# The first block of a fused chunk attention: keys stored once in a row, sums by a column of ones, a new order table

## The chip, the cores and the metric

One core of a Trainium2 chip runs the whole program in one launch. The metric is the device time of one execution in microseconds; three executions of the kernel before give a median of 1080.98 us.

## What is computed

The reference is an attention over chunks, followed by two MLPs, all in float32:

```python
for c in range(768 // 32):
    k_full = concat([mem_k, k[32 * c - 16 : 32 * c + 40]])     # 8 memory keys, up to 56 of the sequence
    v_full = concat([mem_v, v[32 * c - 16 : 32 * c + 40]])
    a = softmax(q[32 * c : 32 * c + 32] @ k_full.T / 8)
    out[32 * c : 32 * c + 32] = a @ v_full
x = out as 3072 tokens x 512
x = silu(x @ w_in) @ w_out            # 512 -> 2048 -> 512
x = relu(x @ w2_in) ** 2 @ w2_out     # 512 -> 2048 -> 512
```

There are 4 batches, 8 heads and a head size of 64. Neighbouring chunks share keys: a chunk sees 16 keys to its left, its own 32, 8 to its right, and the same 8 memory keys as every other chunk of its head.

## The kernel before

**Tiling.** The 3072 tokens are 6 blocks (j) of 512. A block's attention is done in 4 units (p), each of one pair of heads and 16 chunks. The first MLP runs over 16 tiles (i) of 128 hidden units; every float32 matrix is held as a high part and a rest, and three matmuls make one product. Blocks 0 and 1 take the plain form: `hidden` (12 matmuls, L1204 to L1206), silu on ACT, the split of the result, and `back` (12 matmuls, L1263 to L1265). Later blocks and the second MLP use forms with fewer products.

**The start.** Block 0 can't begin its MLP before its four attention units have made x and before the weights of tile 0 have been loaded and converted. A weight tile comes as 64-bit words; `words` (L849) takes them apart with two ACT instructions (L858, L863) and two DVE instructions (L867, L873), then ACT makes the high part (L956) and DVE or POOL the rest (L960). W(i,0) below is the words of tile i of the input matrix, W(i,1) those of the output matrix, 512 KB each.

**A first unit** (`attend_first`, `soften`, `weigh_first`, `norm_first`) works on a pair of heads a = 0, 1 at once. Keys and values lie in block form: a tile of [128 partitions, 2, width], in which partition rows of the other head are zero. So each half is first cleared by a memset (`clear`, L573) and then filled by a DMA over every other partition (`fill_block`, L582). For the keys the width is 16 chunks x 64 = 1024 columns: every chunk has its own copy of all its 64 keys, memory included. For the values it is 16 x 64 = 1024 columns. The sums of the softmax come from 7 small products against a tile `heads` of [128, 2, 2], loaded by a DMA of its own (L547), and are read with the values' results by three DVE instructions (L780 to L784). PE turns the scores and the results by matmuls with an identity `ident`, which has a pool of its own.

**Holding back.** W(1,0), W(2,0) and the raw inputs of block 1 are not loaded at once: a one-column copy on POOL (`room`, L911, L480) writes into their buffers first, and reads x of unit 0 or 1, so that the load waits for that x. All loads are issued by SP, in its program order.

**The order.** Every piece of work is a `Piece` with the engines that may do it. The order of all pieces, and the engine of each (V, A, G for DVE, ACT, POOL), stands in a table written out by hand, `ORDER` (L88): each word is a step in the list of pieces. An engine runs its pieces in that order; waits follow from the data and from buffers that are used again.

Of the kernel before, what the change touches and what calls it, by code (L numbers as in the profile page):

```python
# [12 lines left out]
F32 = mybir.dt.float32  # L13
# [12 lines left out]
GC = 4  # L26
# [19 lines left out]
ZERO = {"DVE": 1.1, "POOL": 1.2, "ACT": 1.0}  # L46
# [42 lines left out]
0V 1 3 11 -10G 2A 1 -2 10V 2A -1 2 -10 11 7G -6A 8A 1 -4 2 -25 7V 2V 1 33G 1 -36 34 -13V -10 1V 1  # L89
56 -32A 1 -35V 23V -12V 31V -22V 1 16A -49A 36 -7 5V 3A 1 17 1A -5A -1 -19 21 41 -31V 1 -24V 1 1A  # L90
23A -22V 43G 1 -7A 1A 38 -70 9 -4V 17V 1 1A -14V 1 1A 49 -28V 1V 1A -22V 40G 1 -18G 244G 1 1G -265
8 -7V 8V 272G -258A -1A 2V 6A -28 27A -19 -7A 1V 322 -301V 302 1 -317A 1V 317 -63 -206 8 -42A 1V
12A -1A 2V 1V -10V 303 -4A 5 -303V 3 232 -192 261 -68V -226A 295 -6A 1V -289G 299 -296A 223V 1V
-237A 51 254A -304G 237V -226A 235 -225A -8V 292A -277A -14V 6A -3 289V -7 -281 -3A 7V 5A 38 -49V
293A -286V 12A 22 250 -278V -5A 6V 280A -274A -11V 47 -29A 268V 2 -282A 6V -4 9A -10V 49 -43V 14A
-1A -7V 204 -209A 199 -185V 261A -2 -272V 199A -151 -43V 9V -8A 2 192 75A -266 -2V 49 -41A 263 -2V
-258A -2G 185V -182A 7A 176V -139 -36A -7V 257 2A -207 -44V -7V 66 -58V -7A 181 77A -257V 260
-253A 251V -178 -79 180A -173G 2A 172V 83 -254A 9A -1A -7V 44 205A -240V 6A -14V 249A -240V 164
-170 19A -18 246V -4 -236A 176 -185A 10G 163V -161A 162V 12 -158A -8A 155V 1V -175G 251A -75 -120
199 -234V 156A -155V -9V 1V 9A 155 -161 235A -228V -9A 234 -70V -153A -10G 164V 73V -218A 1A 220A  # L100
-228V 153 -144V 223 -231V 153A -144V -6 225A -224 150V -153A 228V -4 -212A -11G 12A -4A 5V 7A -11V
10A 136 -141V 12A 15 193 -213V -4 213A -74V 12 -153A 7V 209A -74V -141G 19A 123V 74V -4 -201A 142
-10V -123A -8V -5A 26 -12V 198A -211V 18A 191 -195V 5A -14V 207A -180 -17A 5V -12 -2A 3 204V -197G
120 79 -78A -130V 14V 3 -2A 4A 112 -115V 4A 193 -81V 77A -175 -13V 112V -107A -4V 112 -107A 180
-72A -94 -13V -5A 113V 74A -186G 190A -3V -176A 104 -110V 7A 182 -186 108V -110A 19 -12V 178A -182
108V -110G 215 -104V -100A 174V -173A 169 -69V 76A -163 -18V 182A -176V -5A 182V -181G 10A 94 103
-30 -166A -6V 100A -80 -13V 1V -7A 177 -175 6A -7V 10A -2V 3A 1V 13 74 78A -164V 162 -75V -84 1
-3A 87V 77A -163G 4A 160V -77 -82A 161 -78A -82V 12 -7A 78V -77A -5V 6V -5A 178 -19A -153V 151 33
-30A -159V 6A 172V 12 -30V -153G 3A 169V -168A 169V -18 -154 173V -169V 170A -169V 301V -298 456
-309A -146 166V 132G -131 -170A 150A 27 -176V 458A -308V -4 53 260A -282V 283V -145 -137V -8 9V -8  # L110
-20 29V -8 9A -8 147 -13V 1V 154 -310A 2V 2A -3 29V -27 28 -26 310 -4A 1A -306V 30 280A -3V -306
142G 160 8A -269 -11V 113G 168V -286 119G -118 5V -4 118G -117 4V 281 -167 11A -10 -114 117V 12A
# [12 lines left out]
-112V 10A -9V 5A -3 30V -22A 23V -162 241A -106V 5V 103 -247 5V -4 1 138V -137 287 -284V 144A -4G
100V 2A -97G -144V 242A -97 -7V -137 242V -97A -6G 95 23 -117V 19V -13V 2 -1 -6V 19V -11A 115 3
-2A -102 -13V 116V -265 160V -159 1 159V -158 275 -11A -104 105A 11 -129 109A -108 118V 1V 12 -25A
1V 36 -22A 1V 116 -94 -12V -131A 1G 108A 24V 11 -292A 280V -22G -2G 37 -142 -1 132V 14A -13A 15V
-60 59 -3 1 16 -44V 3A 34 -20V -12A -1G 29A -27V 41 -2A -311V 284 17V 11G 13 -10A -1A 12 -28 18V
1V 10 -86A -3A 1V 5 56 4A 34 1 -33A 13A -1V 10V -86G 143 -78V 33 1 -33A 13A -73A 75A -3G -35 44V  # L130
-20V -23 81 -80 62 -61 42V -8V 9 -26V 37 -93V -4A 1G 108 -22 1 1 1 -33 66A -44V 45V 1 12 -11A 1A
11 -10G -22A 23G 12 1V 11 -22A 13V -14G -25A 162 -113 -21A -33A -2A 45V 2V -13V 2G 30 -9 1 -54A
-1V 2V 4V -8V 47A -11A 1V 21 -49V 39V -29 75 3 12 -60 46A 3A 2V -4V 14 -9V -2A 3V 9 11 -110A -1A
59 53 46 -156V 1V 89A 1G -38A -7A 46A -44A 63 -12V 1V 12 -65G 91 -88A -71A 70V -12 1 1 55A -54 -31
42V 62 -20V 2V 44A 2 1A 1A -3V -160V 173 1 -53V -99G 1V 1V 50A 4A 86V -89V 90V -138 95 55 12 1
-165G 142A 1G -140 95 162 -151A 44V 2V -1V 2V -15V -30A 33A 1V 21 1 -54A -62V 63V -2V 34A 1V -48 1
1 56A 1V -48G 94 3 12 1 -166A 1V 2V -1V 149A 3A 2V -51 9 41A 12 -61 72 1 1 1 -176V 147V -45 -100A
-3G 4G 1 99 1 59V 1V -121A 111A -149A 1V 2 -1 195 -47V -3V -151V 111A 1V 1A 1V 69 -74A 1V 66 -24G
-144A 1V 34V -33 1 144A 1V 1A 27A 2 1A 1A 1G -25V 1 -7V -146A 1V 185 1 3 12 -11V 2V -1V 2V -191 -1
275 -97A 1G -16A 38 -36A -13 1 1 17G 5G 1G -22 -114 161 1 -36A 1G -4V 2V 38 -11A -13A 2A 29 1A 2  # L140
12 1 -11A -33V -2V 13V 19V 2A 2V -61A 1V -111 174A -25 -153A 1A 58 117G 10 1V 1V 1V 1 44 -55G -2G
-175V 161A 1V 33 1 1 1 -33A -164V 165V 12A -15A 1V 15V -176A 1A 1V 175A 26 1A 2 20 1 -20A 1A 22 12
-64V -175V 193 13V -60 -90 127 1 -132A 95 1 1 -148V 2V 199V -149A 1V 196A -248G 207A -2G 21V 1V 1V
21V -247G 206G -25 -179 1 179 158 -104 -29A -15A -2A 47 -10V 1A 10 -44A 57V -200V 140V 2V 15V
-147A 1V 133V -142A 1A 1V 2V 196 -197V 148V 52 12 -210V 1V 195A 3A -48A 49A -48V 59 -58A -210 62
-59 235 31 71 -93V -19V 52 1 1 -34V -19 54 -13V -207A 4A -8G 152G 73 -72A 2A 37V -183G 1 180V -179
215 -69A -3G 58V 15V 3 -74G 73 3 1 -2 -108A 1V 34V 22A -9 1 1 -168V 190V 18V -32V 53 1 -53A -8 54
8 1 -53A 30 -31V -176 -1 179V 53 -39V 3A -2V 1V 2V 1A 1V 58 3 12 1 -73A 1V 57A 3A 2G -1A -3V 5V
# [1910 lines left out]
```

## Time and profile before

| | |
|---|---|
| median of three executions | 1080.98 us (1080.51 to 1084.42) |
| profiled execution, own time | 1079.09 us |
| its span in the profile | 1077.1 us |
| mean granted clock of PE | 0.998 |
| bytes moved by DMA | 257.66 MB |

The span is from the first to the last instruction on the engines; the own time has 1.99 us more around it. PE is the tensor engine's matmuls, PEld its weight loads, DVE, ACT and POOL the other three engines, SP the engine that issues DMAs. The granted clock PEclk is a share of 2.4 GHz. Matmuls are pipelined, so that a busy PE is not one at its peak.

### The profile page before, as it was taken

The page shows a single profiled execution, that of the slowest core. Times are in us where ns is not written, and L with a number is a line of the kernel's source. Part 1 is how long each engine was busy: PE and PEld are TensorE (multiplying, and loading weights), DVE is VectorE, ACT ScalarE, POOL GpSimd, SP SyncE. Part 2 cuts the span into 40 slices and gives each one's busy share as a digit, 9 for nine tenths or more (in the row PEclk, how much of TensorE's full clock was granted, in tenths as well). Part 3 has the DMA queues.
Part 4 walks back from the last instruction along what each step waited for, and adds up shares of the span by engine and source line. Part 5 has one row for each costly group of instructions (what it writes and reads, how often), then busy time and mean ns, then how long its engine had stood idle before and what let it go on. Part 6 is the DMA issues. An engine that isn't in the chain of part 4 may idle for free.

```text
span 1077.1 us, 24974 instructions
## 1 busy us (share of the span) xinstructions
PE 1064.3 (99%) x9857; PEld 976.9 (91%) x9857; DVE 826.7 (77%) x1610; ACT 604.8 (56%) x1110; POOL 252.8 (23%) x232
## 2 busy tenths in 40 slices
PE   7999999999999999999999999999999999999998
PEld 5787777778888888988999999999999999999998
DVE  6877757677978888888888877677777777677766
ACT  4998854556766777767576534335335334335333
POOL 1122123123333333410201231221222123122110
PEclk9999999999999999999999999999999999999999
DMA  8967687979798888786665767667577577567675
GB/s 276 342 216 220 228 283 234 305 232 313 234 303 294 281 279 290 269 310 222 231 210 197 252 207 228 193 210 232 186 214 240 177 210 241 187 203 237 191 222 170
DMA packets 139748, 257.66 MB, mean 239 GB/s; under 512 B 12272, under 2 KB 52336, under 8 KB 139632
## 3 DMA queue, kind: packets, MB, share of 16 engines
q1 hardware_dynamic: 139632, 256.07, 73.1%
q8 instruction: 78, 1.28, 0.5%
q14 instruction: 38, 0.31, 0.1%
HBM read 203.59 MB, written 52.43 MB: 238 GB/s over the span
## 4 chain that ended last, share of the span: by engine, by line
PE 94%; DMA 2%; ACT 1%; SPq 1%; DVE 1%; issue 0%; POOL 0%; ACTq 0%; DVEq 0%; POOLq 0%
PE out L1598 37%; PE pp L1416 22%; PE ph L1204 8%; PE ph L1206 8%; PE ph L1205 8%; PE acc L1263 3%; PE acc L1265 3%; PE acc L1264 2%; PE po L740 1%; PE sc L516 1%; DMA y<-y 1%; DMA i<-weights 1%; DMA blocks<-head 0%; DMA turned<-bounce 0%; PE turned L633 0%
## 5 line engine op out<-in xcount | busy, mean ns | idle before, releaser
L1416 PE MATMUL pp<-xs,forms 128*128 128x256 f32 x2016 | 273.5, 281 | 0.0
L1598 PE MATMUL out<-w,g 128*128 128x256 f32 x2016 | 272.5, 283 | 0.0
L1598 PEld LDWEIGHTS out<-w,g 128*128 128x128 f32 x2016 | 255.6, 191 | 0.0
L1416 PEld LDWEIGHTS pp<-xs,forms 128*128 128x128 f32 x2016 | 253.4, 189 | 0.0
L1474 ACT CAST g<-sums 128x512 fp32r<-128x512 f32 x240 | 147.5, 619 | 122.5 <-PE out L1598 103.9
L1478 DVE TENSOR_TENSOR g<-sums,g 128x512 fp32r<-128x512 f32 x201 | 153.8, 770 | 45.3 <-ACT g L1474 44.1
L1598 PE MATMUL out<-g,w 128*128 128x256 f32 x1344 | 172.0, 283 | 0.0
L1598 PEld LDWEIGHTS out<-g,w 128*128 128x128 f32 x1344 | 166.0, 188 | 4.6
L1433 ACT ACTIVATE sums<-pp 128x256 f32<-128x256 f32 x192 | 73.8, 384 | 165.1 <-PE pp L1416 124.0
L1459 POOL TENSOR_TENSOR sums<-sums 128x256 f32<-128x256 f32 x59 | 50.5, 860 | 274.4 <-DVE sums L1459 220.3
L1204 PE MATMUL ph<-x,i 128*128 128x512 f32 x240 | 95.8, 399 | 1.3 <-DVE xq L751 0.9
L1205 PE MATMUL ph<-x,i 128*128 128x512 f32 x240 | 94.7, 395 | 0.0
L1206 PE MATMUL ph<-x,i 128*128 128x512 f32 x240 | 94.7, 395 | 0.0
L1452 DVE SCALAR_TENSOR_TENSOR sums<-sums 128x256 f32<-128x256 f32 x144 | 69.1, 485 | 25.5 <-ACT sums L1433 23.8
L1459 DVE TENSOR_TENSOR sums<-sums 128x256 f32<-128x256 f32 x181 | 76.2, 439 | 10.3 <-ACT sums L1556 7.5
L1478 POOL TENSOR_TENSOR g<-sums,g 128x512 fp32r<-128x512 f32 x39 | 50.8, 1305 | 107.6 <-ACT g L1474 107.5
L1655 ACT CAST w<-w 128x512 fp32r<-128x512 f32 x100 | 59.5, 619 | 25.5 <-PE out L1598 18.4
L1661 DVE TENSOR_TENSOR w<-w,w 128x512 fp32r<-128x512 f32 x85 | 63.0, 765 | 8.3 <-ACT w L1655 7.6
L1204 PE MATMUL ph<-x,d 128*128 128x512 f32 x144 | 57.6, 400 | 0.0
L1206 PE MATMUL ph<-x,d 128*128 128x512 f32 x144 | 56.8, 395 | 0.0
L1205 PE MATMUL ph<-x,d 128*128 128x512 f32 x144 | 56.8, 395 | 0.0
L1442 DVE TENSOR_TENSOR sums<-pp,sums 128x256 f32<-128x256 f32 x96 | 40.3, 420 | 21.3 <-PE pp L1416 20.4
(140 smaller groups left out, 1568.0 us busy)
## 6 DMA issues: line engine op xcount, KB each, us to landing
w<-w2s SPq DMA_DIRECT2D x120, 512.0 KB, 4.0
w<-w1s SPq DMA_DIRECT2D x32, 768.0 KB, 5.1
w<-w2s SPq DMA_DIRECT2D x96, 256.0 KB, 3.2
wraw<-weights SPq DMA_DIRECT2D x44, 512.0 KB, 5.1
raw<-units SPq DMA_DIRECT2D x20, 768.0 KB, 5.6
w2s<-ws SPq DMA_DIRECT2D x56, 256.0 KB, 3.2
raw<-units SPq DMA_DIRECT2D x20, 520.0 KB, 5.5
bounce<-squares SPq DMA_DIRECT2D x32, 256.0 KB, 3.4
```

Source lines behind the costliest of these rows:

```text
L1204: nc.tensor.matmul(o, w[:, 1, ws], x[:, 0, kt], start=(kt == 0), stop=False)
L1205: nc.tensor.matmul(o, w[:, 0, ws], x[:, 1, kt], start=False, stop=False)
L1206: nc.tensor.matmul(o, w[:, 0, ws], x[:, 0, kt], start=False, stop=(kt == KT - 1))
L1416: nc.tensor.matmul(o[:, at], w[:, a, ws], t[:, c, kt], start=first and kt == 0 and r == 0, stop=kt == 1 and r == 2, skip_group_check=True,)
L1433: nc.scalar.activation(t[:, to], q.bank[bank].tile[:, h], func)
L1452: nc.vector.scalar_tensor_tensor(t, t, 0.0, t, op0=ALU.max, op1=ALU.mult)
L1459: engine[e].tensor_tensor(q.t.tile[:, to], a[0].tile[:, a[1]], b[0].tile[:, b[1]], op=op)
L1474: nc.scalar.copy(take(g, [P, 2, 2, HALF2], F32R, "g2")[:, :, 0], read())
L1478: engine[e].tensor_tensor(t[:, :, 1], read(), f(t[:, :, 0]), op=ALU.subtract)
L1598: nc.tensor.matmul(out_, held[:, ms], moving, start=first and r == 0 and (m == 0 or alone is not None), stop=last and r == 2, skip_group_c ...
L1655: nc.scalar.copy(take(w, [P, m, 2, HALF2], F32R, "w2")[:, :, 0], raw.tile[:, at:at + m])
L1661: engine[e].tensor_tensor(t[:, :, 1], raw.tile[:, at:at + m], f(t[:, :, 0]), op=ALU.subtract)
```

## The change

It lays the first block's keys once in a row, brings the ones back into the values, and brings a new order table.

**Keys.** A unit's keys are one row of 600 columns: 16 left keys, chunk 0, memory, chunk 1, chunk 2, memory, chunk 3, and so on, 8 right keys. A window of 64 columns that starts at 32 c + 8 (c // 2) then holds the 64 keys of chunk c, in an order that depends on whether c is even; the rows of the values are put in the same order by the host.

**Values.** Each chunk has 65 columns, the last of them the ones: 1040 columns a half. The seven small products, the tile `heads` and its DMA go. The results go to two banks of 4 x 65 columns each, in place of one of values and one of sums, and `norm_first` reads them with five DVE instructions in place of three.

**Places.** The identity lies in a buffer of the tag y, the queries of unit 0 in that of o9 (a later weight tile).

```diff
-ZERO = {"DVE": 1.1, "POOL": 1.2, "ACT": 1.0}
+KEYS = LEFT + 2 * UC * CHUNK + RIGHT + UC * NMEM
+CLEAR = ({"DVE": 0.70, "POOL": 0.70, "ACT": 0.65}, {"DVE": 1.08, "POOL": 1.07, "ACT": 0.97})
...
-    ident = pool("cst").tile([P, P], F32, name="ident")
+    corner = G.buf("y")
+    ident = take(corner, [P, P], F32, "ident")
...
-    heads = G.buf("rv")
-
-    def load_heads(e):
-        nc.sync.dma_start(out=take(heads, [P, 2, 2], F32, "heads"), in_=head[0, :, -4:])
-
-    G.add({"SP": 0.48}, 5.0, load_heads, new=[heads], size=P * 16)
...
-        got, width = [], KW * 2
-        c0 = 2 * QW + what * width
+        got, width = [], (KEYS, 2 * VW)[what]
+        c0 = 2 * QW + what * KEYS
...
-        return q_blocks.setdefault(p, G.buf("y") if p < 2 else G.buf(("wr", "rq")[p - 2]))
+        return q_blocks.setdefault(p, G.buf(("o9", "y", "wr", "rq")[p]))
...
-                rows = slice(c % GC * CHUNK, (c % GC + 1) * CHUNK)
+                rows, at = slice(c % GC * CHUNK, (c % GC + 1) * CHUNK), c * CHUNK + c // 2 * NMEM
                 nc.tensor.matmul(
                     t[rows, c // GC], qs.tile[:, c * CHUNK:(c + 1) * CHUNK],
-                    k[:, :, c * KC:(c + 1) * KC].rearrange("p a k -> p k a"),
+                    k[:, :, at:at + KC].rearrange("p a k -> p k a"),
...
         def weigh_first(e):
-            o, s = take(po[0], [P, UG, 2, D], F32, "po"), take(po[1], [P, UG, 2], F32, "sums")
+            for b in po:
+                take(b, [P, UG // 2, 2, D + 1], F32, "po")
...
-                    o[rows, c // GC], pts.tile[:, c * CHUNK:(c + 1) * CHUNK],
-                    v[:, :, c * D:(c + 1) * D], start=True, stop=True,
+                    po[c // UC].tile[rows, c // GC % 2], pts.tile[:, c * CHUNK:(c + 1) * CHUNK],
+                    v[:, :, c * (D + 1):(c + 1) * (D + 1)], start=True, stop=True,
                 )
-            for c in range(GC):
-                rows = slice(c * CHUNK, (c + 1) * CHUNK)
-                nc.tensor.matmul(
-                    s[rows, 0], pts.tile[:, rows], heads.tile[:, c > 0], start=True, stop=True
...
+            for at, o in zip(places, made):
+                nc.vector.tensor_scalar(s[:, at], o[:, :, D], EPS, 1.0, op0=ALU.add, op1=ALU.mult)
+            nc.vector.reciprocal(s, s)
+            for at, o in zip(places, made):
+                nc.vector.tensor_tensor(
+                    t[:, at], o[:, :, :D], s[:, at].unsqueeze(2).to_broadcast([P, UG, D]),
+                    op=ALU.mult,
                 )
```

**The order table**, read out into names. S, T, O, B are a unit's scores, turn of the scores, weighing of the values, turn back; h(i,k) is the part of `hidden` of tile i that needs x of unit k; A is the score of block 1's first unit; q, K, V are the loads of queries, keys and values of a unit (a = 0 or 1 behind the point).

```
PE before: S0 S1 T0 S2 O0 T1 T2 B0 S3 O1 T3 B1 O2 O3 B2 B3 h(0,0-3) h(1,0) h(1,1) A h(1,2) h(1,3) h(2) back(0)
PE after:  S0 S1 S2 T0 T1 O0 S3 T2 B0 O1 T3 O2 B1 O3 B2 h(0,0) h(0,1) B3 h(0,2) h(0,3) h(1,0-3) A h(2) back(0)
SP before: q0 q1 K0.1 K0.0 K1.0 K1.1 K2.1 q2 K2.0 heads V0.1 K3.0 V0.0 q3 V1.0 V1.1 W(0,0) K3.1 V2.1 V3.0
           V2.0 V3.1 W(0,1) W(1,0) W(3,0) W(1,1) W(2,0)
SP after:  q0 q2 K0.0 K0.1 q1 K1.0 K1.1 K2.0 K2.1 W(0,0) V0.0 V0.1 K3.1 q3 K3.0 V1.1 V1.0 V2.0 V2.1 V3.0
           V3.1 W(0,1) W(3,0) W(1,0) W(1,1) W(2,0)
clears before: ACT K0.1 K1.1 V1.0 K2.1 K3.1 V3.0 ... V3.1; DVE K1.0 V0.0 V0.1 V2.0 V1.1 ... V2.1; POOL K0.0 K2.0 K3.0
clears after:  ACT K3.1 V1.0 V1.1; DVE K0.1 K1.0 K1.1 K3.0 V0.1; POOL K0.0 K2.0 K2.1 V0.0 V2.0 V2.1 V3.0 V3.1
```

ACT before runs its first two exponentials and only later the words of W(0,0); after, the words of W(0,0) stand ahead of the first exponential. After the start the order on PE differs in 25 places, by neighbours that change places, the last of them the 112th of PE's 1053 pieces: there the weighing of block 2's last unit stands ahead of back(14) and back(15) of block 1, and h(9), which stood between them, behind both. On DVE, between a y copy (L1303) of block 1 and the normalising (L749 to L751) of block 3's first unit, stood two sums (L1459), a rest (L1661) and a sum; after, an x rest (L841), a transpose (L639) and a rest (L1661) stand there. Apart from the clears 59 pieces change between DVE and POOL, 34 of them to POOL, 57 of the 59 beside the first 375 pieces of PE.

## Rows read from the trace of the kernel before

**Rows 1.** The page, part 1: busy us (share of the span) xinstructions.
```profile
PE 1064.3 (99%) x9857; PEld 976.9 (91%) x9857; DVE 826.7 (77%) x1610; ACT 604.8 (56%) x1110; POOL 252.8 (23%) x232
```

**Rows 2.** Busy us by stretch: length, PE, PEld, DVE, ACT, POOL, PEclk, DMA share, GB/s.
```profile
0.00:5.00 5.00, 3.55 (x9) 1.19 (x9) 3.44 (x5) 4.09 (x4) 2.49 (x8) 1.00 0.42 117
5.00:9.00 4.00, 1.77 (x34) 1.00 (x32) 2.06 (x3) 3.06 (x5) 0.95 (x1) 1.00 0.88 286
9.00:12.00 3.00, 2.43 (x35) 2.08 (x36) 1.36 (x3) 0.00 (x0) 0.00 (x0) 0.50 0.99 342
12.00:20.00 8.00, 5.70 (x109) 4.64 (x111) 4.85 (x9) 3.45 (x6) 0.18 (x1) 0.98 0.95 335
20.00:30.00 10.00, 8.41 (x179) 7.77 (x172) 7.15 (x15) 5.28 (x10) 1.89 (x5) 1.00 0.94 310
30.00:37.50 7.50, 7.13 (x90) 4.92 (x89) 6.71 (x12) 6.63 (x12) 1.61 (x2) 1.00 0.85 321
37.50:1070.00 1032.50, 1031.58 (x9387) 951.82 (x9387) 797.56 (x1561) 582.26 (x1077) 244.38 (x215) 1.00 0.73 238
```

**Rows 3.** Chain that ended last, 0 to 60 us: start, length, what.
```profile
9.68 4.92 DMA blocks<-head
...
18.69 0.50 ACT x L838
...
19.91 7.35 DMA i<-weights
...
35.77 1.45 POOL i L960
...
37.26 0.50 PE ph L1204
```

**Rows 4.** Tile blocks, 0 to 30 us: ns min/median/max, first and last start.
```profile
L578 ACT ACTIVATE blocks<-ident x7: 1039/1039/1055, 2.2 to 17.6; 128x1024 f32<-128x1024 f32 x7
L580 DVE MEMSET blocks<- x6: 912/912/912, 1.6 to 13.1; 128x1024 f32 x6
```

**Rows 5.** DMA issues of 0 to 30 us: count, KB each, us to landing.
```profile
blocks<-head SPq DMA_DIRECT2D x16, 256.0 KB, 4.8
```

**Rows 6.** Timeline of PE, 7 to 45 us: start, length, what, idle before.
```profile
7.18 1.30 PE L608 MATMUL sc<-blocks,raw 128*32 128x128 f32 x32 [1.71 <-DMA blocks<-head]
9.57 1.93 PE L608 MATMUL sc<-blocks,raw 128*32 128x128 f32 x32 [1.09 <-DMA blocks<-head]
...
24.34 1.08 PE L762 MATMUL po<-blocks,pts 128*32 128x128 f32 x32
25.23 0.22 PE L768 MATMUL sums<-heads,pts 128*32 128x2 f32 x8
...
26.14 1.08 PE L762 MATMUL po<-blocks,pts 128*32 128x128 f32 x32
...
34.49 0.86 PE L516 MATMUL sc<-raw 64*32 64x64 f32 x64
...
40.16 0.39 PE L1263 MATMUL acc<-g,o 128*128 128x512 f32 x1
```

**Rows 7.** Timeline of DVE, 12 to 20 us.
```profile
16.66 0.17 DVE L780 TENSOR_SCALAR sm<-sums 128x8 f32<-128x8 f32 x1 [1.34 <-PE sums L772]
...
17.10 0.69 DVE L784 TENSOR_TENSOR xq<-po,sm 128x512 f32<-128x512 f32 x1
```

**Rows 8.** Timeline of ACT, 27 to 36 us.
```profile
27.34 0.66 ACT L863 ACTIVATE wr<-i 128x512 int32<-128x512 uint32 x1 [1.73 <-DMA i<-weights]
...
31.52 0.62 ACT L956 CAST i<-wu 128x512 fp32r<-128x512 f32 x1 [0.84 <-DVE wu L873]
...
33.29 1.28 ACT L1223 ACT_TABLE_LOAD   x1
...
35.08 0.61 ACT L956 CAST i<-wu 128x512 fp32r<-128x512 f32 x1
```

**Rows 9.** Timeline of PE, 239 to 256 us.
```profile
249.97 0.47 PE L1204 MATMUL ph<-x,i 128*128 128x512 f32 x1 [0.89 <-DVE xq L751]
```

More of the change, by code (lines that the diff above doesn't have):

```diff
@@ L275 @@
+-17G 14 -13A 17V -3 -13G 17V 7 -6V 7 -6V 2 5 -6V 2 5 -4 5V 2V -1 2
 """
@@ L401, in table @@
         nc.scalar.activation(take(early, [P, UG], F32), ident[:, :UG], AF.Exp)
-    G.add({"ACT": 0.2}, -50.0, table, new=[early], table="exp")
+    G.add({"ACT": 0.2}, -50.0, table, new=[early], uses=[corner], table="exp")
     def keep(e):
@@ L556, in first_place @@
             b = first_places[p, 0][0] if tag == "x1" and what else G.buf(tag)
-            first_places[p, what] = b, what if tag == "x1" else None
+            first_places[p, what] = b, what * KEYS if tag == "x1" else None
         return first_places[p, what]
@@ L574, in clear @@
                 if new:
-                    take(b, [P, *[2] * (slot is not None), 2, width], F32, "blocks")
+                    take(b, [P, 2, width + (0 if slot is None else 2 * VW)], F32, "blocks")
                 if e == "ACT":
@@ L583, in fill_block @@
                 nc.sync.dma_start(out=place()[a::2, a], in_=head[p, a::2, c0:c0 + width])
-            d = G.add(ZERO, due - 2, clear, new=[b] * new, uses=[b] * (not new))
+            d = G.add(CLEAR[what], due - 2, clear, new=[b] * new, uses=[corner] + [b] * (not new))
             d.behind += [b.by] * (not new)
@@ L705, in soften @@
         if on_pe:
-            d = G.add({"PE": 0.55 if j else 0.8}, due - 9 * far, lambda e: turn(e, pt, pr), done, new=[pt],
-                      uses=[pr])
+            d = G.add({"PE": 0.55}, due - 9 * far, lambda e: turn(e, pt, pr), done, new=[pt],
+                      uses=[pr, corner])
             d.matmuls = UG * (j == 0)
@@ L792, in weigh_values @@
         if at is None:
-            if j == 0:
-                val, ready = [*val, heads], [*ready, heads.by]
-            d = G.add({"PE": 0.9 if j else 1.4}, due - 6 * far, weigh, ready, new=po,
+            d = G.add({"PE": 0.9 if j else 0.95}, due - 6 * far, weigh, ready, new=po,
                       uses=[pts, *val])
-            d.matmuls = (4 * UC + 2 * (UG + 3)) * (j == 0)
+            d.matmuls = 4 * UC * (j == 0)
         else:
@@ L803, in weigh_values @@
             sm = G.buf("sm")
-            done = [G.add({"DVE": 1.2}, due - 5, lambda e, sm=sm: norm_first(e, sm), [d],
+            done = [G.add({"DVE": 1.5}, due - 5, lambda e, sm=sm: norm_first(e, sm), [d],
                           new=[sm, xq], uses=po)]
@@ L811, in weigh_values @@
         if on_pe:
-            done = [G.add({"PE": 0.55 if j else 0.8}, due - 3 * far, lambda e: turn(e, back, xq), done,
-                          new=[back], uses=[xq])]
+            done = [G.add({"PE": 0.55}, due - 3 * far, lambda e: turn(e, back, xq), done,
+                          new=[back], uses=[xq, corner])]
             done[0].matmuls = UG * (j == 0)
@@ L2021, in _head @@
     q, k, v = u[..., :QW], u[..., QW:QW + KW], u[..., QW + KW:]
-    v = v.reshape(HP, P, 2, UC, D + 1)
-    inside = np.zeros((HP, 2, D, 2, 2), np.float32)
-    for a in range(2):
-        inside[:, a, :, :, a] = v[:, a * D:(a + 1) * D, 0, :2, D]
-    parts = (q, k, v[..., :D], inside)
+    k, v = k.reshape(HP, P, 2 * UC, KC), v.reshape(HP, P, 2 * UC, D + 1).copy()
+    memory, own = k[:, :, 0, :NMEM], k[..., NMEM + LEFT:NMEM + LEFT + CHUNK]
+    keys = [k[:, :, 0, NMEM:NMEM + LEFT]]
+    for c in range(2 * UC):
+        keys += [memory] * (c % 2) + [own[:, :, c]]
+    keys.append(k[:, :, -1, KC - RIGHT:])
+    at = np.arange(KC)
+    for odd, m in enumerate((LEFT + CHUNK, LEFT)):
+        order = np.concatenate([at[NMEM:NMEM + m], at[:NMEM], at[NMEM + m:]])
+        rows = v[:, :, odd::2].reshape(HP, 2, KC, UC, D + 1)[:, :, order]
+        v[:, :, odd::2] = rows.reshape(HP, P, UC, D + 1)
+    parts = (q, *keys, v)
     rows = np.concatenate([x.reshape(HP, P, -1) for x in parts], axis=-1)
```

385 lines of the change are left out of this document (185 added, 200 removed).

## The prediction

> **What bounds the kernel now.** Read the page's first part, then the busy time by stretch, then the chain that ended last. PE is busy 1064.3 of 1077.1 us [rows 1], so the question is where the other 12.8 us lie. From 37.5 to 1070 us PE idles 0.92 us in all, in the first 37.5 us 8.5 [rows 2]; the remaining 3.4 us lie in the last seven. Nothing in the diff removes work behind the start, so a gain there can come only from the 0.92 us; I leave the last seven as they are. What is left is the moment from which PE is fed without a break: it is 37.26 us, where h(2), the hidden matmuls of tile 2, begin [rows 3]. The set of PE pieces ahead of h(2) is the same in both orders, so the end moves by as much as h(2) does, as long as what follows keeps up.
>
> What holds h(2)? The chain says it: a load of blocks of 4.92 us, the first unit, x on ACT at 18.69, and then the held W(1,0), 7.35 us from 19.91 to 27.26 us, ten more microseconds of conversion on ACT, DVE and POOL, and PE at 37.26 [rows 3]. Meanwhile the DMA engines are busy 0.94 to 0.99 of the time from 9 to 30 us, at 310 to 342 GB/s; but in the first 5 us only at 0.42 [rows 2]. So the start is bound by supply, and behind it by the conversion; PE has time to spare there: 2.30 us idle of 8.00 from 12 to 20 us and 1.59 of 10.00 to 30 us [rows 2].
>
> **The change part by part.**
>
> *Bytes.* A block load carries 64 rows of 1024 columns, 256 KB [rows 5]. A key load falls to 600 columns, 262 to 154 KB (thousands of bytes): eight times 108.5 is 868 KB less. A value load grows by 16 columns, 4.1 KB, eight times 33 KB. Net 835 KB less, the load of heads aside, which is 2 KB. At 310 to 335 GB/s [rows 2] that is 2.5 to 2.7 us of supply.
>
> *Order of the loads.* W(0,0) moves ahead of the values, and W(3,0) ahead of W(1,0). All loads are on one queue. Up to and with W(1,0) SP has issued 6.81 MB before and 6.50 MB after: W(3,0), 524 KB, takes back most of the saving at this point, and 0.31 MB remain.
>
> *An earlier start.* In the first 5 us 585 KB move (5 x 117) [rows 2]. SP waits there for clears: the load of K0.1 needs the one that ACT begins at 2.2 us and makes in 1.04; DVE takes 0.91 and begins at 1.6 [rows 4]. After, DVE clears K0.1 first, 600 of 1024 columns, 0.53 us, ready at 2.1; K0.0 is POOL's first as before. If DMA runs at the 310 GB/s of later from 2 us on, it has moved 930 KB by 5 us: a lead of 345 KB. The bounds are none of it and all of it. I take all, since five clears and nine loads stand ready by then: SP stops only at V0.1, whose clear stands on DVE behind that of K3.0, which waits for the end of the warm-up matmuls (5.47, S0's start less PE's wait [rows 6]); I put that clear's end at 7.1 us, and by then some 2.5 MB are issued and 1.6 MB moved, so the wait is covered.
>
> *W(1,0).* 0.31 and 0.345 MB at 310 GB/s make it land 2.1 us earlier, at 25.1 us. Its hold gives the same: x of unit 0 comes in my walk at 17.2 to 17.8 us in place of 18.69, and the row's 7.35 us behind that give 25.2. Bounds: 27.3 us (nothing gained) and 22.7 us (the 4.92 us of the blocks' load in the same chain [rows 3] behind 17.8). I take 25.1, as the queue is as full as before.
>
> *The walk to x of unit 0.* S0 starts at 7.18 us, after 1.71 us of waiting for its blocks [rows 6]; after, at 5.5, with the end of the warm-up. S1 and S2 follow their loads, by bytes at 7.7 and 9.0 us. The new wait is on ACT: the words of W(0,0) stand ahead of the first exponential, by bytes they land near 11 us, two instructions of 0.66 us [rows 8], and the exponential begins at 12.3; behind it queue all of ACT's work of the start. O0 begins at 12.9, where the row of the chain has 14.6 (9.68 and 4.92) [rows 3], and B0 near 16.5.
>
> *Sums.* Weighing takes 0.89 us (24.34 to 25.23) and the small products 0.91 (25.23 to 26.14) [rows 6]; four times 0.91 is 3.6 us less PE work, and the 130 columns for 128 add 0.01 each. On the path it is hidden by the waits above but for the one unit between O0 and B0. The normalising pays part back: one more instruction of 0.17 us, and the one of 0.69 us in two parts [rows 7], which cost between nothing and 0.69 more; I take 0.15, 0.3 us a unit with the first.
>
> *Conversion behind W(1,0).* Before, ACT starts on it at 27.34, waits 0.84 us for DVE at 31.52, and makes tile 2's high part at 35.08 [rows 8]; POOL ends the rest 1.45 us from 35.77, h(2) follows at 37.26: 10.0 us behind the landing [rows 3]. After, two x copies are no longer in the pile (one done before it, one moved up), and the join of tile 1 no longer makes ACT wait, since two pieces of W(0,1) and x of unit 3 lie between. ACT's six instructions from 27.34 to 30.68 start 0.56 us apart [rows 8]. By that I count, in ACT's new order, tile 1's high part 2.8 us behind the landing, 0.6 long, its rest on POOL to 4.85 (1.45 [rows 3]), then h(1) with 2.9 us (as h(2), 37.26 to 40.16) and A with 0.8 [rows 6]: 8.55. Tile 2 gives nearly the same: two words, the silu table load and silu (1.8 us, 33.29 to 35.08 [rows 8]), the high part to 7.0, the rest on POOL to 8.4. So 8.55 us, bounds 8.0 and 10.0.
>
> h(2) then starts at 25.1 + 8.55 = 33.65 us, 3.6 us earlier. back(0) needs the rest of W(0,1), by the same count 11.2 us behind the landing; h(2) ends at 11.45, so PE doesn't stop there, with little to spare.
>
> *The order behind the start.* PE's one wait of 0.89 us, up to 249.97 us [rows 9], is for a bank that DVE's normalising of block 3's first unit frees. Before, DVE has two sums on it, one rest of weights and one more sum between its y copy and this normalising; after, the sums are gone, but an x rest, a transpose and a rest of weights stand there. That is four instructions against three, near 2 us either way, so I take the wait as kept: nothing. Bounds: gone (0.9 us of gain) or grown (rival 3).
>
> The sum: 3.6 us. The profiled execution took 1079.09 us, 1.99 more than its span; 3.6 less is 1075.5. The median stands 1.89 us above it, so 1077.4.
>
> *A rule of the Trainium skill.* In the rows PE's granted clock is 0.50 from 9 to 12 us, that is 1.2 GHz in place of 2.4, after PE had waited 1.71 and 1.09 us; S1 took 1.93 us there, S0 1.30 [rows 2, 6]. "TensorE: Matmul & The Clock Gate", part 1, says that the slow clock is the default and activity releases it; the change takes activity out of the start. By that rule the start would be slower than my walk; by the rows it is a matter of three microseconds. It is rival 2.
>
> **The rivals.**
>
> 1. *The start gives the gain back.* Only W(1,0)'s 2.1 us come through, the conversion still takes 10 us, or W(0,0) lands later and the first exponential with it. For it: ACT's pile is the same work. Against it: the 0.84 us wait goes. Gain 1 to 2 us: about 1079.5.
>
> 2. *The slow clock through the start, on the other side.* After, gaps of a microsecond stand between S0, S1, S2 and O0, and each unit has 0.9 us less to do. If 1.2 GHz held from S1 to x, PE work would become the bound: 10.5 us of scores, turns and weighing at 1.93/1.30, the 5.6 us of h(0) and h(1) at twice their time, A 1.2: 28 us from 7.7, with the 2 to 4 us of waits that remain: h(2) at 37.7 to 39.7, later than 37.26. It decides once h(2) is later than 37.26 us. About 1083. Against it: before, the clock was back at 0.98 from 12 to 20 us with PE 71% busy [rows 2].
>
> 3. *A new wait between 37.5 and 300 us.* 34 pieces go to POOL, where the rest of a tile took 1.45 us [rows 3]; the first pair of block 2 gets three such in a row. A bank or a split that comes late stops PE, whose order is fixed. Price: several times the 0.89 us; from 3.6 us on it eats the gain: 1080 to 1088.
>
> 4. *More than forecast.* W(1,0) lands at 23 us; then the last turn back at 24 and tile 1 bind, and h(2) starts near 31.7, 5.5 us earlier; with the wait of 249.97 gone 6.4: 1074.6.
>
> That the change doesn't do what it says can be seen in the diff for the bytes and the products; it can't be a rival here.
>
> **How the numbers follow.** Forecast 0.56, rival 1 0.20, rival 2 0.08, rival 3 0.06, rival 4 0.10. A measurement of this kernel tells about 0.5% from no change, 5.4 us: below 1075.6 is faster, above 1086.4 slower. The forecast's own range is 1074.5 to 1079.5 (W(1,0) and conversion within 2 us, the wait gone or kept); a third of it lies below 1075.6, 0.19, with rival 4 0.29. Slower: half of rival 3 and a little of rival 2, 0.05. Same: 0.66. The range of 8 in 10 takes in rival 4 and rival 1 and the nearer half of rivals 2 and 3: 1073 to 1082.
>
> **What would show it.** Right: S0 at 5.5 us; DMA share above 0.8 from 2 us on; W(1,0) landed by 25 us; h(2) at 33 to 34 us and no idle PE from there to 240 us; one wait of about 0.9 us near 246 us. Wrong: a granted clock of 0.5 beyond 12 us, an exponential of unit 0 later than 14 us, or PE waits for weight tiles between 34 and 60 us, which would mean that the supply, and not the start, now sets the time.

## The result, and the profile after

| | before | after |
|---|---|---|
| median, six executions each | 1080.93 us | 1070.84 us (1068.28 to 1072.01) |
| ratio after to before | | 0.9900, 95% interval 0.9882 to 0.9918 |
| profiled execution, its span | 1077.1 us | 1066.4 us (own time 1068.28, the fastest of the six) |

The kernel is 10.1 us faster by the medians. Forecast were 3.6 us, and a range that ended at 1073: the result lies below it.

First the page, part 1, and the busy time by stretch of the kernel after; they answer to [rows 1, 2].

```profile
PE 1054.6 (99%) x9801; PEld 972.8 (91%) x9801; DVE 828.4 (78%) x1608; ACT 600.1 (56%) x1106; POOL 266.0 (25%) x246
```

```profile
0.00:5.00 5.00, 3.55 (x9) 1.16 (x9) 2.16 (x4) 0.00 (x0) 4.44 (x12) 1.00 0.57 164
5.00:9.00 4.00, 2.89 (x66) 2.00 (x64) 2.87 (x4) 3.60 (x4) 2.41 (x3) 1.00 0.98 305
9.00:12.00 3.00, 1.75 (x40) 1.51 (x38) 1.77 (x3) 0.85 (x2) 0.00 (x0) 1.00 0.91 294
12.00:20.00 8.00, 7.15 (x154) 5.63 (x156) 7.13 (x21) 3.95 (x9) 1.46 (x2) 1.00 1.02 383
20.00:30.00 10.00, 7.44 (x61) 5.36 (x62) 7.29 (x16) 7.96 (x14) 1.70 (x4) 1.00 0.95 348
```

The start did what the change says: more is moved early (164 GB/s in place of 117), DMA then reaches 383 GB/s, and PE's granted clock stays at 1.00 from 9 to 12 us, where it was 0.50. The timelines of ACT and PE, which answer to [rows 6, 8]:

```profile
11.45 0.68 ACT L841 ACTIVATE wu<-i 128x512 f32<-128x512 f32 x1 [2.15 <-DMA i<-weights]
...
23.18 0.66 ACT L841 ACTIVATE wu<-i 128x512 f32<-128x512 f32 x1 [0.96 <-DMA i<-weights]
```

```profile
5.96 1.29 PE L601 MATMUL sc<-blocks,raw 128*32 128x128 f32 x32 [0.64 <-DMA blocks<-head]
...
13.28 1.09 PE L756 MATMUL po<-blocks,pts 128*32 128x130 f32 x32 [0.70 <-ACT pts L682]
...
31.66 0.50 PE L1187 MATMUL ph<-x,i 128*128 128x512 f32 x1
```

S0 starts at 5.96 us, O0 at 13.28, W(1,0) has landed at 23.18, and h(2) starts at 31.66 in place of 37.26 [rows 3]: 5.6 us earlier in this execution. Behind it PE's waits up to 410 us, from 245 us on (the table of waits: us in total, times, longest):

```profile
PE out L1581 <- POOL g L1461: 0.4, 1, 0.4
PE out L1581 <- DVE g L1461: 0.2, 1, 0.2
```

The 0.89 us of [rows 9] are gone and small new waits have come. That leaves some 5 of the 10.7 us between the two spans, in a part of the kernel where PE is busy all the time in both. There the matmuls themselves are quicker. The same lines, first before, then after (busy us, mean ns of one). `ph<-x,i` is `hidden`: PE holds a tile of i, which PEld has loaded as weights, and moves x through it. `out<-w,g` belongs to the forms with fewer products, whose matmuls, pp and out, have 256 columns:

```profile
L1598 PE MATMUL out<-w,g 128*128 128x256 f32 x2016 | 272.5, 283 | 0.0
...
L1205 PE MATMUL ph<-x,i 128*128 128x512 f32 x240 | 94.7, 395 | 0.0
```

```profile
L1581 PE MATMUL out<-w,g 128*128 128x256 f32 x2016 | 273.4, 283 | 0.1
...
L1188 PE MATMUL ph<-x,i 128*128 128x512 f32 x240 | 93.8, 391 | 0.5 <-DVE x L824 0.5
```

Nothing in the diff touches these lines, yet a matmul of 512 columns takes 4 ns less. The spans of neighbours overlap, so what counts is the step from one start to the next. It shows in a timeline: the first and the last of the same 12 matmuls `back`, before and after.

```profile
55.54 0.39 PE L1263 MATMUL acc<-g,o 128*128 128x512 f32 x1
...
58.09 0.40 PE L1265 MATMUL acc<-g,o 128*128 128x512 f32 x1
```

```profile
49.88 0.39 PE L1246 MATMUL acc<-g,o 128*128 128x512 f32 x1
...
52.38 0.39 PE L1248 MATMUL acc<-g,o 128*128 128x512 f32 x1
```

Eleven steps take 2.55 us before and 2.50 after, 232 and 227 ns. Over all 1536 matmuls of 512 columns the medians of the step are the same two numbers; 1536 times 5 ns is 7.7 us. The 5376 matmuls of 256 columns give a part back: their busy time is 2.3 us more. Counted along PE's sequence, the kernel after leads by 5.6 us at h(2), by 11.7 at the last matmul of 512 columns (578.21 and 566.48 us) and by 10.6 at the end.

What else differs for these matmuls? Where their operands lie. The value tiles have grown from 8192 to 8320 B per partition, three of them (u0 to u2), so every buffer placed behind them, x and g among them, has moved by 384 B. The byte at which a buffer starts in its partition, from the two programs:

```
                                    before   after    modulo 256
i0 (and all of i, d, o: weights)      1152    1152    128, 128
x0 (moved by ph)                    156928  157312      0, 128
first g (moved by acc)              189696  190080      0, 128
```

My theory, "places": the step goes by the distance of the moving tile from the held one, modulo 256: 128 before, 0 after. The rival: other engines' and DMA's traffic, which the new order has changed. Below, a distance is the moving tile's place less the held tile's, and each step is a median over the trace.

### The profile page after: what moved, and what is told of

The parts are those of the page before. It is cut to its first block, busy times and chain, and to the rows that moved or that the text cites. A ratio compares the mean times of both kernels' runs of the same rounds, so it can differ in the third digit from the quotient of the medians.

```text
span 1066.4 us, 24883 instructions
## 1 busy us (share of the span) xinstructions
PE 1054.6 (99%) x9801; PEld 972.8 (91%) x9801; DVE 828.4 (78%) x1608; ACT 600.1 (56%) x1106; POOL 266.0 (25%) x246
## 4 chain that ended last, share of the span: by engine, by line
PE 93%; DMA 2%; DVE 1%; ACT 1%; POOL 1%; issue 0%; SPq 0%; ACTq 0%; DVEq 0%; POOLq 0%
PE out L1581 36%; PE pp L1399 22%; PE ph L1187 8%; PE ph L1188 8%; PE ph L1189 8%; PE acc L1246 3%; PE acc L1248 3%; PE acc L1247 3%; PE sc L515 1%; PE po L733 1%; DMA i<-weights 1%; DMA xf<-y 1%; DMA w2s<-ws 0%; PE turned L626 0%; POOL blocks L573 0%; DMA raw<-units 0%
## 5 line engine op out<-in xcount | busy, mean ns | idle before, releaser
L1442 POOL TENSOR_TENSOR sums<-sums 128x256 f32<-128x256 f32 x68 | 59.9, 884 | 296.8 <-DVE sums L1442 246.3
L1187 PE MATMUL ph<-x,i 128*128 128x512 f32 x240 | 94.9, 395 | 2.0 <-ACT x L821 1.3
L1188 PE MATMUL ph<-x,i 128*128 128x512 f32 x240 | 93.8, 391 | 0.5 <-DVE x L824 0.5
L1189 PE MATMUL ph<-x,i 128*128 128x512 f32 x240 | 93.5, 390 | 0.0
L1442 DVE TENSOR_TENSOR sums<-sums 128x256 f32<-128x256 f32 x172 | 71.0, 432 | 5.5 <-ACT sums L1539 4.5
L1644 DVE TENSOR_TENSOR w<-w,w 128x512 fp32r<-128x512 f32 x88 | 62.4, 734 | 11.7 <-ACT w L1638 10.9
L1187 PE MATMUL ph<-x,d 128*128 128x512 f32 x144 | 57.1, 396 | 0.0
L1187 PEld LDWEIGHTS ph<-x,i 128*128 128x128 f32 x240 | 45.1, 188 | 12.3 <-ACT x L821 1.8
L1188 PE MATMUL ph<-x,d 128*128 128x512 f32 x144 | 56.2, 390 | 0.0
```

The costliest lines, as they stand in the source:

```text
L1187: nc.tensor.matmul(o, w[:, 1, ws], x[:, 0, kt], start=(kt == 0), stop=False)
L1188: nc.tensor.matmul(o, w[:, 0, ws], x[:, 1, kt], start=False, stop=False)
L1189: nc.tensor.matmul(o, w[:, 0, ws], x[:, 0, kt], start=False, stop=(kt == KT - 1))
L1442: engine[e].tensor_tensor(q.t.tile[:, to], a[0].tile[:, a[1]], b[0].tile[:, b[1]], op=op)
L1644: engine[e].tensor_tensor(t[:, :, 1], raw.tile[:, at:at + m], f(t[:, :, 0]), op=ALU.subtract)
```

## The experiments

**Places, without the order.** An unused tile ahead of rq, a buffer that lies between u2 and x, moves x and g on by 128 B in the kernel after, to the distance of before (a1), and by 384 B in the kernel before, to the places of after (b1):

```diff
 a1: the kernel after
+    pool("pad")
...
+    pools["pad"].tile([P, 32], F32, tag="pad", name="pad")
 b1: the kernel before, ident in y and q0 in o9 as in the change
+    pool("pad")
...
+    pools["pad"].tile([P, 96], F32, tag="pad", name="pad")
...
```

> The changed kernel with one unused tile of 128 B per partition ahead of the buffer rq: every buffer behind it lies 128 B further on, the x tiles and g at 256 B past a multiple of 512 (as in the kernel before) in place of 128. Order, data and instructions are those of the changed kernel. Theory 'places': the 512-column matmuls, 227 ns from start to start in the changed kernel and 232 in the one before, depend on where their moving tile lies; the step goes back to about 232 ns and the kernel takes some 5 us more, about 1076. Rival 'order and traffic': the step comes from what the other engines and DMA do beside the matmuls; it stays at 227 ns and the time at 1071.

> The kernel before with its identity in a y buffer and the queries of unit 0 in o9 (as in the change), and an unused tile of 384 B per partition ahead of rq, so that the x tiles, g and all behind them lie at the addresses of the changed kernel. Order table, data and products are those of the kernel before. Theory 'places': the step of the 512-column matmuls falls from 232 to 227 ns, h(2) stays at 37.3 us, the time falls by some 5 us to about 1076. Rival 'order and traffic': 232 ns and 1081 us as before.

Measured: a1 1077.41 us, 0.9967 of the kernel before (0.9953 to 0.9981), step 232 ns; b1 1076.02 us, 0.9965 (0.9950 to 0.9980), step 227 ns. The lines of a1, then of b1:

```profile
L1191 PE MATMUL ph<-x,i 128*128 128x512 f32 x240 | 94.9, 395 | 0.5 <-DVE x L827 0.5
```

```profile
L1209 PE MATMUL ph<-x,i 128*128 128x512 f32 x240 | 93.8, 391 | 0.0
```

The step follows the places in both directions and doesn't care for the order table, the data or what DMA does: the rival falls. At the old places the change is worth 0.33%, 3.6 us (2.1 to 5.1 by the interval); the places are worth 0.67% in the kernel after and 0.35% in the kernel before. In b1 part of it is given back, as PE, being earlier, meets waits, 3.1 us in all from 245 to 410 us, where the kernel before has 0.9. Its table of waits:

```profile
PE out L1602 <- POOL g L1482: 1.0, 1, 1.0
PE po L744 <- ACT sums L1560: 0.9, 2, 0.6
PE ph L1208 <- DVE sm L753: 0.6, 1, 0.6
PE ph L1208 <- DVE xq L755: 0.6, 1, 0.6
```

**Data and order apart.** c1 is the kernel after with the order table of before (its load of heads taken out); d1 is the kernel before, with ident in y and q0 in o9, and the order table of after.

```diff
 c1: the kernel after
 ORDER = """
-0V 3 22 -21G 1 1V ...
+0V 1 2 11 -10G 2A ...
 d1: the kernel before, ident in y and q0 in o9
 ORDER = """
-0V 1 3 11 -10G 2A ...
+0V 4 22 -21G 1 1V ...
```

> The changed kernel (short keys, ones in the values, its buffers) with the order table of the kernel before, without its load of heads. If the start's gain is the bytes alone, h(2) comes near 32 to 34 us and the time stays within 2 us of the changed kernel's; if it is the order of loads and clears, h(2) comes at 35 to 37 us and the time rises by 3 to 5 us to 1074 to 1076. For the step of 512-column matmuls: theory 'places' says 227 ns (the addresses are the changed kernel's), rival 'order' says 232.

> The kernel before (blocks of 1024 columns, small products, its load of heads; identity in y and queries of unit 0 in o9, every other address its own) with the order table of the changed kernel, the load of heads put ahead of the first value block. 868 KB more are loaded and W(3,0) still stands ahead of W(1,0), so by bytes at 310 GB/s W(1,0) lands 2.7 us later than in the changed kernel, near 26, and h(2) comes at 34 to 35 us; if the order alone makes the start, it comes at 32. For the step of 512-column matmuls: theory 'places' says 232 ns and a time of 1077 to 1079; rival 'order' says 227 ns and 1072 to 1075.

Measured: c1 1070.75 us, 0.9913 (0.9893 to 0.9933), step 227 ns, h(2) at 34.84; d1 1077.96 us, 0.9985 (0.9969 to 1.0001), step 232 ns, h(2) at 36.94. c1's time is the one expected of the bytes alone, its h(2) lies near the one expected of the order; d1's h(2) is 2 us later than expected. By the start of one profiled execution each, the data are worth 2.4 us, the order 0.3, and both together 5.6. That they pay more together is not shown: ten traces with both (listed further down) have h(2) 2.5 to 5.6 us ahead of the kernel before, and d1 lost time to PE's clock. Its chain (start, length, what) shows both the small products and h(1), of which seven matmuls in a row step at 0.43 us in place of 0.23; the granted clock was 0.50 from 32 to 34 us:

```profile
20.47 0.76 PE sums L766 x6
...
22.77 0.76 PE sums L766 x6
...
25.07 0.76 PE sums L766 x6
25.83 0.51 PE turned L627 x4
26.36 0.59 ACT x L832
26.95 0.57 ACT wu L852
...
32.18 0.43 PE ph L1199
...
35.76 0.23 PE ph L1199
```

The new order brings the weights early: ACT doesn't wait for W(1,0) at 26.95. Then PE's own work up to the last x is the chain, and the small products stand on it, once per unit (at a clock of 0.65 from 12 to 16 us, which lengthens this work too). With the old order it is not the chain: in c1 the held W(1,0), 6.95 us from 22.61, is. The rate of DMA seems to go with the order: from 12 to 20 us d1 moves 382 GB/s, as after, c1 326; but e2 below, with the new order, moves 343. In the total c1 and the kernel after can't be told apart, though their h(2) lie 3.2 us apart. Most of that is the choice of execution: the profiled one of the kernel after (1068.28 us) is 2.6 us faster than its median, that of c1 (1070.52) 0.2.

**Which distance.** Four more places, the kernel after but for these (e1: 64 B and e4: 32 B ahead of rq; e3: 128 B between x1 and g; e2 moves rv):

```diff
 e1
-        ("rq", 1), ("rv", 2), ...
+        ("pad", 1), ("rq", 1), ("rv", 2), ...
+    pools["pad"].tile([P, 16], F32, tag="pad", name="pad")
 e2
-        ("rq", 1), ("rv", 2), ("pr", 1), ("pts", 1), ("xq", 3), ("x0", 1), ("x1", 1), ("g", 3), ("wraw", 2),
+        ("rq", 1), ("pr", 1), ("pts", 1), ("xq", 3), ("x0", 1), ("x1", 1), ("g", 3), ("rv", 2), ("wraw", 2),
```

> The changed kernel with an unused tile of 64 B per partition ahead of rq: x and g at 192 past a multiple of 512. The theory 'places' as run a1_pad128 left it says only that 128 is fast (227 ns) and 256 slow (232 ns). If what counts is that the moving tile lies as the weights do (they lie at 128 in every kernel), 192 is slow: 231 to 232 ns, about 1076. If 256 is a bad place of its own, 192 is fast: 227 ns, 1071.

> The changed kernel with the two rv buffers (8320 B) placed behind g instead of ahead of the x tiles: x0, x1 and g lie at a multiple of 512, pr, pts and xq too. If only the same place as the weights' (128) is fast, the step is 231 to 232 ns and the time about 1076. If 256 alone is bad, or if any place that is a multiple of 512 suits 2-KB rows, the step is 227 ns or less and the time 1071 or less.

> The changed kernel with an unused tile of 128 B per partition between x1 and g: the x tiles stay at 128, g and all behind it lie at 256. Theory 'places, of the moving tile itself': the hidden matmuls, which move x, keep 227 ns, and the matmuls back, which move g, go to 232 ns; about a third of the 512-column matmuls are slower, 2 us in all, 1073. Rival 'places, of something else behind g' (raw words, work and split tiles of the other engines and DMA): both kinds go to 232 ns, 1076, or both stay.

> The changed kernel with an unused tile of 32 B per partition ahead of rq: x and g at 160. If the step goes by whole multiples of 64 or 128 B, or by an exact match with the weights' place, it is 231 to 232 ns; if it grows with the distance, between 227 and 232. Time 1071 to 1076 accordingly.

| run | distance of x, of g | step of ph, of back | time, ratio (interval) |
|---|---|---|---|
| e1 | 64, 64 | 229, 229 ns | 1062.06 us, 0.9823 (0.9799 to 0.9847) |
| e2 | -128, -128 | 232, 232 ns | 1074.95 us, 0.9936 (0.9913 to 0.9959) |
| e3 | 0, 128 | 227, 232 ns | 1071.88 us, 0.9922 (0.9898 to 0.9946) |
| e4 | 32, 32 | 234, 234 ns | 1071.42 us, 0.9912 (0.9893 to 0.9931) |

e3 separates it best: x and g differ in place, and so do ph and back, in one kernel; it is the moving tile's own place. e2 says that a round address is no merit. e4's 234 ns lies above all that was expected of it. e1 is the surprise: its steps of 512 columns are a little longer than after, and the kernel is 8 us faster still (0.9823 against 0.9900). Its lines show where:

```profile
L1583 PE MATMUL out<-w,g 128*128 128x256 f32 x2016 | 273.4, 283 | 0.1
L1401 PE MATMUL pp<-xs,forms 128*128 128x256 f32 x2016 | 265.9, 278 | 0.4 <-DVE kept L1427 0.4
L1583 PE MATMUL out<-g,w 128*128 128x256 f32 x1344 | 168.3, 280 | 0.4 <-DVE g L1463 0.3
```

The matmuls of 256 columns whose operands now lie 64 apart (most of pp; out with g moving) have 12.7 us less busy time than after. The median step of pp is 114 ns in place of 120; of out with g moving half of the steps are at 113 to 114 and most others at 117 to 119. The form of out with w moving, where w and g were shifted together and the distance is still 0, keeps 120. So far it seemed that 512 columns want a distance of 0 and 256 columns one of 64. e4 is slower with 512 columns and quicker with 256, and ends where the kernel after does.

**The distance by itself.** m1 has nothing but matmuls: one held and one moving tile that lie equal modulo 256 (the moving one 256 off modulo 512), both read at 0, 64, 128 and 192 B further on; 48 matmuls of 512 and 48 of 256 columns for each of the 16 pairs.

> Matmuls alone: of the kernel's work nothing is left, the output is a block of products. One held tile and one moving tile lie equal modulo 256; both are read at 0, 64, 128 and 192 B further on, in all 16 pairs, with 48 matmuls of 512 columns and 48 of 256 columns for each pair, while no other engine works and no DMA runs. From the kernels so far I read: the step goes by the distance of the moving tile from the held one modulo 256. 512 columns: 227 ns at a distance of 0, 229 at 64, 232 at 128, 233 at 192. 256 columns: 120 ns at 0, 114 at 64 and 192, 119 at 128. Theory 'places': this grid shows the same, along its diagonals. Rival 'contention with the other engines and DMA', that the distance only decides who else is met: all 16 pairs agree within 1 ns, at 226 and 113.

Five groups of its timeline, from the held tile at 64 and the moving one at 0 on; a group's steps are the next start less its own, over 48:

```profile
86.30 11.36 PE L34 MATMUL o<-x,w 128*128 128x512 f32 x48
97.50 5.61 PE L39 MATMUL o<-x,w 128*128 128x256 f32 x48
102.94 11.06 PE L34 MATMUL o<-x,w 128*128 128x512 f32 x48
113.84 5.92 PE L39 MATMUL o<-x,w 128*128 128x256 f32 x48
119.59 11.37 PE L34 MATMUL o<-x,w 128*128 128x512 f32 x48
```

At 64 and 0: 233 and 113 ns; both at 64: 227 and 120; then 64 and 128 begins. All sixteen, read in this way, for 512 / 256 columns:

```
            moving 0     64          128         192
held 0     227 / 120   233 / 118   232 / 119   233 / 118
held 64    233 / 113   227 / 120   233 / 118   232 / 119
held 128   232 / 120   233 / 113   227 / 120   233 / 118
held 192   229 / 118   232 / 119   233 / 118   227 / 120
```

No other engine works here and no load or store runs, so contention with them falls as a cause. The diagonal is firm, 227 and 120; so is a distance of 128 (232; 119 to 120). At 64, 512 columns have 233 in three pairs, where it is 320 modulo 512, and 229 in the one where it is 64 there too, as in e1. At the odd multiples of 64 I expected 113 or 114 for 256 columns throughout, and found 113 in two pairs and 118 in six.

**From the rule to a faster kernel.** f1 puts 64 more bytes between g and the raw words, f2 moves x0 ahead of u0 as well, f3 gives the kernel before the places of f2.

```diff
 f1: e1 and
-        ... ("g", 3), ("wraw", 2),
+        ... ("g", 3), ("pad2", 1), ("wraw", 2),
 ...
 f2: f1 and
-    for tag in ("u0", "u1", "u2"):
+    for tag in ("x0", "u0", "u1", "u2"):
 ...
```

> The changed kernel with 64 unused bytes ahead of rq (run e1_pad64) and 64 more between g and the raw words: in the second layer the moving w2 in wraw and wu and the held g then lie 64 apart in place of 0. By 'places' 1728 matmuls of 256 columns go from 120 to 114 ns: 10 us less than e1_pad64's 1062, near 1052. Rival 'it is the absolute place, and 192 is a good one for wraw': 1062 or more.

> As f1_two_pads, with x0 placed ahead of u0, so that x0 lies 0 from the weights of the first layer (227 ns for 576 matmuls in place of 229) and 64 from g (288 matmuls of 256 columns at 114 in place of 120). By 'places' 1.2 and 1.7 us less than f1_two_pads, near 1049. If another engine takes over as the bound, PE waits show between 250 and 400 us or behind 600 us and the time stays at 1052.

> The kernel before (its blocks, products and order table; identity in y, queries of unit 0 in o9) with its buffers placed as in f2_x0_first, by three unused tiles. If the change itself, without its addresses, is worth the 3.6 us that run a1_pad128 leaves for it, this stands 3 to 6 us above f2_x0_first, near 1054. If the two effects are not separate, it is 1060 or more.

Measured: f1 1064.40 us (0.9856, 0.9841 to 0.9871), f2 1064.36 us (0.9863, 0.9848 to 0.9878), f3 1066.77 us (0.9883, 0.9867 to 0.9899). The first two miss by 12 and 15 us, and are no faster than e1. In f1 nearly all of the second layer lies 64 apart, and nearly all of it steps at 118 ns, pp too, whose places are those of e1:

```profile
L1402 PE MATMUL pp<-xs,forms 128*128 128x256 f32 x2016 | 271.3, 280 | 1.1 <-DVE kept L1428 1.1
L1584 PE MATMUL out<-w,g 128*128 128x256 f32 x2016 | 269.1, 280 | 0.1
```

So there are two steps for one distance, 113 and 118, and the place alone doesn't choose. f3 is the kernel before at 0.988: nearly all that the change brought comes without the change. Between f2 and f3, at like places, 2.4 us are left for the change itself, less than the 3 to 6 expected; their intervals overlap, so that this is not clear of noise.

**What chooses between 113 and 118.** m2 is m1 with groups in a row at chosen distances, its two tiles equal modulo 512; g1 is e1 with x0 ahead of u0, g2 is e1 with 64 B between wraw and wu.

> Matmuls alone, of the kernel's work nothing is left. 256-column matmuls (then 512-column ones) in groups of 24 to 72, one held tile, the moving tile 0, 64, 128, 192 or 32 B from it, in an order that puts groups at 64 behind groups at 0, at 128, at 192, at 32 and behind a pause. Theory 'what ran before': at a distance of 64 the step is 113 ns behind a group at 0 and stays so through the group; behind a group at 128 or 192, or behind a pause, it is 118 and stays 118. Rival 'place alone': every group at 64 has the same step. For 512 columns both say 227 at 0; by the first theory the step at 64 is 229 behind 0 and another value (233) behind 128.

> As e1_pad64, with x0 placed ahead of u0: x0 at a distance of 0 from the first layer's weights (576 matmuls of 512 columns at 227 in place of 229 ns, 1.2 us) and of 64 from g (288 matmuls of 256 columns). Matmuls of the raw words w2 in wraw and wu against g stay at 0 and so keep the others of the second layer at 113 to 114 ns. By 'what ran before': 1 to 3 us less than e1_pad64, near 1060. Rival, that f1_two_pads and f2_x0_first were slower for another reason than the missing groups at 0: 1062 or more.

> As e1_pad64, with 64 unused bytes between wraw and wu: of the raw words against g, those in wraw (1152 matmuls) stay at a distance of 0, those in wu (576) go to 64. If the groups at 0 that are left still bring the others to 113: 576 times 6 ns, 3.5 us less than e1_pad64, near 1058.5. If two groups at 64 in a row, with pauses between, lose it, the second layer goes to 117 to 118 as in f1_two_pads: 1063 to 1064.

Medians of m2, each group named by its distance, in the order in which they ran:

```
256 columns:  0 120 | 64 118 | 128 119 | 64 118 | 0 120 | 64 118 | pause | 64 118 | 0 120 | 64 118 | 192 118 | 64 118
              0 120 | 192 113 | 0 120 | 32 119 | 64 118 | 0 120 | 64 118
512 columns:  0 227 | 64 229 | 128 232 | 64 229 | 0 227 | 192 233 | 0 227 | 64 229
```

512 columns: here the step goes with the place, whatever ran before. That the 233 of m1's three pairs comes from 320 modulo 512 doesn't hold, though: in f3 g and half of the x tiles lie at 320 from their held tiles, and step at 229. 256 columns: at 192 the step is 118 behind a group at 64 and 113 behind one at 0, at one and the same place. So what ran before may count, which one group of each kind in one execution can't tell from chance; it doesn't count as I put it, since 64 gives 118 in every group. g1 takes 1061.64 us (0.9827, 0.9802 to 0.9851) and g2 1061.78 us (0.9835, 0.9807 to 0.9863): neither can be told from e1, and the 1 to 3.5 us expected of them did not come. What decides between the two steps stays open. e1 and g1, 1.7 to 1.8% under the kernel before, are the fastest versions found; they beat both kernels.

## Why the prediction was wrong, point by point

**The step that failed** stands in its first paragraph: "Nothing in the diff removes work behind the start, so a gain there can come only from the 0.92 us". No work was removed there, and the time fell all the same. I read the page's 99% of PE as a fixed amount of work; its matmuls have a price of their own, which goes with addresses, and the diff moves addresses by widening a tile. At the old places (a1) the kernel takes 1077.41 us, and by its ratio 3.6 us less than before: the predicted gain. That it is just this number is in part luck: in a1's profiled execution h(2) starts 4.4 us earlier than before, and PE then loses some of it to a wait of 2.0 us, behind which its clock is 0.85 from 330 to 340 us. The missing 6 to 7 us are the places (a1 against after: 0.9967 and 0.9900); what in the chip makes the step go by them stays open.

**Bytes and start: right in the main, in part by luck.** h(2) was forecast for 33.65 us. Ten traces with this data and order (after, a1, e1 to e4, f1, f2, g1, g2) have it between 31.66 and 34.80, with a median of 33.9; the profiled execution of the kernel after is the earliest. There W(1,0) landed at 23.18 in place of 25.1, and the conversion behind it took 8.48 us, where 8.55 were counted. The hold ended at 17.44 us, as walked; what was too long is the load behind it, 7.35 us taken over from the kernel before:

```profile
17.44 5.72 DMA i<-weights
```

The forecast counted with a full clock. The three traces that have one up to h(2) (after, a1, g1) start h(2) at 31.66 to 32.87, earlier than forecast; the seven with a stretch of slower clock at 33.49 to 34.80. The two errors offset each other near 33.65.

**The small products**: said to be hidden but for one. In the kernel before, the chain holds one unit's; with the new order and the old data (d1) it holds all four. What their going is worth there was not measured apart.

**The wait at 249.97**: taken as kept; it went, and 0.4 and 0.2 us came nearby. Nearly nothing either way, as summed.

**The rivals.** The slow clock did not come in the profiled execution: 1.00 from 9 to 12 us. It came in d1, 0.90 there and 0.82 from 12 to 20 us, after PE had been busy for 1.40 of the 4 us up to 9 us; in the kernel after it was busy for 2.89 of them. The rule of the Trainium skill ("TensorE: Matmul & The Clock Gate", part 1: slow by default, released by activity) agrees with both rows; what I had wrong was that the change would take activity out ahead of 9 us, since S1 now follows S0 after 0.47 us. But a clock of 0.5 beyond 12 us, a sign of being wrong, came in seven of the ten traces, at other places than rival 2 had it: in f1 and f2 between 16 and 20 us, in e1 to e4 and g2 between 26 and some 34 us, in h(1). PE had been busy there for 1.1 to 2.0 of the 4 us from 24 to 28; but for 1.4 in the kernel after, where the clock stayed. In e2 it was 0.50 from 28 to 32 us, and over the whole start 0.91:

```profile
0.00:37.50 37.50, 30.13 (x397) 20.99 (x398) 24.86 (x50) 20.80 (x34) 13.69 (x23) 0.91 0.86 297
```

In none of the ten is h(2) later than 37.26, so rival 2's price was too high. Of the six executions of the kernel after, too, only the profiled one has a mean clock of 1.000; the others have 0.996 to 0.998 and take 2.2 to 3.7 us longer, though no trace shows where theirs fell. A new wait of rival 3's kind shows in a1, a rest of g on POOL:

```profile
PE out L1584 <- POOL g L1464: 2.0, 1, 2.0
```

Rival 4 had the start of the profiled execution (31.7 us, the wait gone) and with 1074.6 us was still 3.8 too high: no case of mine held the matmuls' own step.

## What to carry to other kernels

Before a change to a tile's width is costed, list which buffers it moves: a matmul's step is part of the profile, and here 384 bytes were worth more than 835 KB. Where PE is the bound, read the step from start to start by shape, against the places of its held and moving tiles modulo 256; an unused tile of 64 B is the cheapest experiment there is. And when a change and its measurement disagree, undo its side effects one at a time before its purpose is explained anew.

## What was not expected of the hardware

With a weight load before each matmul, 512 float32r columns step at 227 ns when held and moving tile lie 0 apart modulo 256, 229 at 64 (233 in three of m1's pairs), 232 at 128, 233 at 192 and 234 at 32; 256 columns at 120 at 0, 113 or 118 at 64 and 192, 119 at 128. All but the 234, and the 113 at 64, also stand with every other engine at rest and no load or store under way.

The Trainium skill, "SBUF — State Buffer", section "A bandwidth-pool intuition that's wrong (but worth ruling out)", gives PE a second, independent read port for weight loads. By that one would expect no effect of the distance; the grid of m1 differs by it, 227 against 233 ns, and the measurement decides. "TensorE: Matmul & The Clock Gate", section "Back-to-back issue gap", gives 512 columns some 131 ns each in a stream with weight loads, for no stated type; in no run here is the median step of 512 float32r columns under 227.
